# A shorter VectorE program in a grouped-query decode attention kernel: 119 VectorE instructions fewer

## The chip, the cores and the metric

One core of one Trainium2 chip. The metric is the device time of one execution in microseconds (us); lower is better. The profile's span of the same execution is about 2 us shorter than this time, so spans are compared with spans and times with times. The program runs on one core, and all runs told here were in the fast state.

## The reference, cut to what matters

```python
B, Hq, Hkv, Sq, Sk, D = 1, 32, 8, 1, 65536, 128     # bf16
k = repeat(k, 4, axis=1); v = repeat(v, 4, axis=1)   # 4 query heads share one K/V head
scores = einsum("bhqd,bhkd->bhqk", q, k) * D ** -0.5
out = einsum("bhqk,bhkd->bhqd", softmax(scores), v)
```

One query row per head attends to 65,536 keys. K and V together are 268 MB, each byte is used once, and all else is small.

## The kernel before

A "group" g is one of the 8 K/V heads with its 4 query heads. Its K and its V come in two tiles b of 8.4 MB. SBUF holds three tiles at a time: buffer 0 for V, buffers 1 and 2 for the two K tiles of a group. SyncE issues the loads in a fixed order, each behind a wait for the buffer's last reader:

```python
    def load_k(g, b):
        SP.wait((s_sc, 16 * g - 8 + 8 * b if g else 0))   # score matmuls of the old tile are done
        ...  load(k, g, b, 1 + b, ...)
    def load_v(g, b):
        done = 2 * (2 * g + b)
        ...                                               # the last V tiles come in pieces
        else:
            SP.wait((s_vc, done))                         # value matmuls of the old tile are done
            load(v, g, b, 0, s_v[0])
    ...
    for g in range(1, G):
        for b in range(2):
            load_k(g, b)
            load_v(g - 1, b)
```

VectorE transposes each K tile in place, takes the maximum of the scores, prepares the softmax and gathers the result of the group before:

```python
    def transposes(g, b):
        for t0 in range(0, SL, PS):                       # SL = 256, PS = 64: four per tile
            ...
            dve.transpose(out=part.bitcast(u32), in_=part.bitcast(u32)).then_inc(s_kt, 2)
            yield
    def bank_max(g, b):                                   # four per group, 512 columns each
        DV.wait((s_sc, 16 * g + 4 * b + 4))
        return DV.mark(dve.tensor_reduce(out=mx[:, b:b + 1], in_=sc[:, 512 * b:512 * b + 512], ..., op=ALU.max))
    def collect(g):
        n = DV.mark(dve.tensor_scalar_mul(out=vs[:, 0:D], in0=vacc[:, 0, :], scalar1=sely[:, 0:1]))
        ...                                               # copy of the exp sums
        for y in range(1, 4):
            DV.after(n)
            n = DV.mark(dve.scalar_tensor_tensor(out=vs[:, 0:D], in0=vacc[:, y, :], scalar=sely[:, y:y + 1], in1=vs[:, 0:D], ...))
        ...                                               # memset of vacc
    def finish(g):                                        # reciprocal, scaling, a store of 1 KB
        d_rl = reciprocal(pf[0:H, D:D + 1], 3 * g + 7)
        ...
        act.dma_start(out=out[0, g * H:(g + 1) * H, 0, :], in_=o[:, :]).then_inc(s_st, 16)

    for g in range(G):
        ...  # transposes(g, 0); transposes(g, 1) with weights(g - 1, 1) and two bank_max inside
        bank_max(g, 2); DV.after(bank_max(g, 3)); top(); softmax(g)
        if g: DV.wait((s_vc, 4 * g)); collect(g - 1)
        weights(g, 0)
        if g: finish(g - 1)
```

TensorE runs one loop over tiles x = 2g + b: the score matmuls of tile x (8 parts, each behind a share of the transposes), then the value matmuls of tile x - 2, and after each second tile the two small transposes of the softmax.

## Time and profile before

| | before |
|---|---|
| time, median of 3 runs before the prediction (6 with those taken later) | 630.77 us (631.06) |
| loading queue's packets, share of 16 DMA engines' span | 98.9% |
| VectorE busy | 346.9 us, 55% |
| TensorE busy (modelled) | 350.6 us, 56% |

The page of the profile of the kernel before, cut. The row "DMA" has the busy share of the 16 DMA engines in 40 equal slices, in tenths. In the groups below it the last columns are busy us and mean ns of one instruction, then the engine's idle time before them and what ended it.

```profile
span 629.4 us, 6741 instructions
...
PE 350.6 (56%) x2136; PEld 138.0 (22%) x2136; DVE 346.9 (55%) x236; ACT 31.3 (5%) x25; POOL 7.4 (1%) x39
...
DMA  8999999999999999999999999999999999999996
GB/s 367 433 466 400 466 400 463 404 462 404 458 408 458 408 462 404 466 400 467 400 466 400 466 400 466 400 463 404 462 404 462 404 462 404 428 436 433 431 424 248
...
q1 hardware_dynamic: 6624, 268.44, 98.9%
...
q14 instruction: 2, 0.02, 0.0%
...
L225 DVE STREAM_TRANSPOSE io<-io 128x4096 uint32<-128x4096 uint32 x64 | 279.8, 4417 | 152.2 <-DMA io<-in_k_dram 152.2
...
L230 DVE TENSOR_REDUCE mx<-sc 128x1 f32<-128x512 f32 x32 | 20.8, 668 | 48.2 <-PE sc L395 48.2
...
L278 DVE SCALAR_TENSOR_TENSOR vs<-vacc,sely,vs 128x128 f32<-128x128 f32 x24 | 8.4, 351 | 0.6
...
```

The DMA row stands at 9 from the second slice to the last but one: the core is loading all the time. VectorE waits 152.2 us for K tiles, that is, it is ready before its input is there.

The chain of waits that ended last, cut: start, duration, what.

```profile
...
609.60 13.11 DMA io<-in_v_dram
...
622.76 1.45 PE vacc L360 x8
624.21 0.87 PE pf L454 x8
...
625.11 1.38 PE pf L454 x16
...
626.82 0.36 ACT o L323
```

The end of the program hangs on the last V load. After it come 4.5 us of matmuls and a copy, and then the last store.

What could make a slower computing engine cost time is the loading queue running dry (in wide256, below, it does, and the time is 660.02 us). That is read from the timeline, here in the middle of the program (start, duration, engine, line, what; in brackets the idle time before). SPq lines are the issues of loads.

```profile
...
281.98 1.90 PE L360 MATMUL vacc<-io,et 128*16 128x512 bf16 x32
282.09 0.69 DVE L230 TENSOR_REDUCE mx<-sc 128x1 f32<-128x512 f32 x1 [5.74 <-PE sc L395]
...
282.81 0.16 DVE L235 TENSOR_REDUCE mg<-mx 128x1 f32<-128x4 f32 x1
...
286.09 0.33 SPq L132 DMA_DIRECT2D io<-in_v_dram  x1
...
294.65 17.42 DVE L225 STREAM_TRANSPOSE io<-io 128x4096 uint32<-128x4096 uint32 x4 [1.62 <-DMA io<-in_k_dram]
...
300.23 9.55 PE L395 MATMUL sc<-io,wz 128*128 x32 [7.83 <-issue]
...
323.97 0.33 SPq L132 DMA_DIRECT2D io<-in_v_dram  x1
...
333.36 8.77 DVE L225 STREAM_TRANSPOSE io<-io 128x4096 uint32<-128x4096 uint32 x2 [21.28 <-DMA io<-in_k_dram]
...
```

The V load is issued at 286.09, and the K load in flight then has landed at 294.65, when its transposes start: 8.6 us of margin. The next V load is issued at 323.97, and the K load ahead lands at 333.36: 9.4 us.

### The profile page before, as it was taken

What the parts mean: (1) busy time and instruction counts of PE and PEld (TensorE: products, weight loads), DVE (VectorE), ACT (ScalarE), POOL (GpSimd) and SP (SyncE); (2) the same over time, 40 slices, a digit from 0 to 9 for tenths busy, and PEclk for the clock granted to TensorE, in tenths of its full rate; (3) what the DMA queues carried; (4) which work ended last, traced back from release to release, by engine and by line L of the source; (5) the groups of instructions that cost most, each with busy time, mean ns of one, the idle gap of its engine ahead of it and who ended that gap; (6) DMA issues with size and microseconds to landing.
All of it is one profiled execution on the core that took longest, in us unless ns stands there. A gap on an engine that the chain in (4) does not pass through costs nothing. (4 is left out here: it accounts for less than half of the span.)

```text
span 629.4 us, 6741 instructions
## 1 busy us (share of the span) xinstructions
PE 350.6 (56%) x2136; PEld 138.0 (22%) x2136; DVE 346.9 (55%) x236; ACT 31.3 (5%) x25; POOL 7.4 (1%) x39
## 2 busy tenths in 40 slices
PE   0676582736627375372854719457184571886435
PEld 0222130312213122130321303123031230332102
DVE  4993926649066590765808567084670947684200
ACT  0000100020000200002000020000200002000100
POOL 1000000000000000000000000000000000000000
PEclk9999595977959779697896968869698696999577
DMA  8999999999999999999999999999999999999996
GB/s 367 433 466 400 466 400 463 404 462 404 458 408 458 408 462 404 466 400 467 400 466 400 466 400 466 400 463 404 462 404 462 404 462 404 428 436 433 431 424 248
DMA packets 6739, 268.49 MB, mean 427 GB/s; under 512 B 848, under 2 KB 1104, under 8 KB 1488
## 3 DMA queue, kind: packets, MB, share of 16 engines
q1 hardware_dynamic: 6624, 268.44, 98.9%
q10 hardware_dynamic: 112, 0.02, 0.0%
q8 instruction: 1, 0.02, 0.0%
q14 instruction: 2, 0.02, 0.0%
HBM read 268.44 MB, written 0.01 MB: 427 GB/s over the span
## 5 line engine op out<-in xcount | busy, mean ns | idle before, releaser
L395 PE MATMUL sc<-io,wz 128*128 x1024 | 268.2, 412 | 205.7 <-PEq L114 108.9
L225 DVE STREAM_TRANSPOSE io<-io 128x4096 uint32<-128x4096 uint32 x64 | 279.8, 4417 | 152.2 <-DMA io<-in_k_dram 152.2
L395 PEld LDWEIGHTS sc<-io,wz 128*128 x1024 | 104.8, 102 | 369.2 <-issue 290.9
L360 PE MATMUL vacc<-io,et 128*16 128x512 bf16 x1018 | 70.9, 411 | 21.6 <-PEq L114 20.2
L230 DVE TENSOR_REDUCE mx<-sc 128x1 f32<-128x512 f32 x32 | 20.8, 668 | 48.2 <-PE sc L395 48.2
L249 ACT ACTIVATE ex<-sc,nmb 128x2048 bf16<-128x2048 f32 x8 | 15.8, 1969 | 560.9 <-DVE nmb L247 560.9
L360 PEld LDWEIGHTS vacc<-io,et 128*16 128x16 bf16 x1018 | 27.4, 94 | 60.0 <-issue 35.5
L266 DVE STREAM_TRANSPOSE et<-ex 128x512 bf16<-128x512 bf16 x32 | 20.6, 681 | 16.6 <-PE vacc L360 14.2
L354 PE MATMUL pf<-vs,sel 128*4 128x129 f32 (+1 forms) x20 | 5.7, 386 | 42.0 <-PEq L114 42.0
L239 DVE TENSOR_REDUCE m<-pt 1x4 f32<-1x128 f32 x8 | 2.2, 278 | 30.8 <-PE pt L438 30.8
L257 ACT ACTIVATE sc<-zero 128x2048 f32<-128x2048 f32 x7 | 13.2, 1882 | 0.3
L340 POOL COPY wz<-qT 32x16 bf16<-32x16 bf16 x32 | 6.1, 191 | 516.5 <-PE sc L395 454.3
L354 PEld LDWEIGHTS pf<-vs,sel 128*4 128x4 f32 x20 | 1.2, 83 | 42.4 <-issue 42.4
L273 DVE TENSOR_SCALAR vs<-vacc,sely 128x128 f32<-128x128 f32 x8 | 2.7, 343 | 13.5 <-PE vacc L360 13.5
L422 PE MATMUL pt<-et 128*16 128x512 bf16 x32 | 9.7, 384 | 0.0
L278 DVE SCALAR_TENSOR_TENSOR vs<-vacc,sely,vs 128x128 f32<-128x128 f32 x24 | 8.4, 351 | 0.6
L270 DVE RECIPROCAL rl<-pf 4x1 f32<-4x1 f32 x7 | 1.0, 149 | 10.0 <-PE pf L354 10.0
L440 PE MATMUL pb<-one,nrow 1*128 1x1 f32 x8 | 1.6, 196 | 5.7 <-PEq L114 5.7
L284 DVE MEMSET vacc<- 128x512 f32 x7 | 3.4, 485 | 1.3 <-DVE vs L278 1.3
L422 PEld LDWEIGHTS pt<-et 128*16 128x16 bf16 x32 | 3.0, 93 | 4.1 <-issue 0.6
L247 DVE COPY nmb<-pb 128x1 f32<-128x1 f32 x8 | 1.3, 159 | 3.0 <-PE pb L440 3.0
L438 PE MATMUL pt<-ident,mg 128*1 128x128 f32 x8 | 2.3, 282 | 1.1 <-PEq L114 1.1
(30 smaller groups left out, 22.3 us busy)
## 6 DMA issues: line engine op xcount, KB each, us to landing
io<-in_v_dram SPq DMA_DIRECT2D x5, 4096.0 KB, 16.1
io<-in_k_dram SPq DMA_DIRECT2D x4, 4096.0 KB, 26.0
io<-in_k_dram SPq DMA_DIRECT2D x4, 2048.0 KB, 39.0
io<-in_v_dram SPq DMA_DIRECT2D x1, 2048.0 KB, 11.0
io<-in_v_dram SPq DMA_DIRECT2D x1, 1024.0 KB, 13.1
io<-in_v_dram SPq DMA_DIRECT2D x3, 256.0 KB, 13.5
io<-in_v_dram SPq DMA_DIRECT2D x2, 128.0 KB, 13.4
io<-in_k_dram SPq DMA_DIRECT2D x13, 47.2
```

What stands on the lines that cost most here:

```text
L225: dve.transpose(out=part.bitcast(u32), in_=part.bitcast(u32)).then_inc(s_kt, 2)
L230: return DV.mark(dve.tensor_reduce(out=mx[:, b:b + 1], in_=sc[:, 512 * b:512 * b + 512], axis=AX.X, op=ALU.max))
L249: n = ACTQ.mark(act.activation(out=ex[:, :, :].rearrange("p b n -> p (b n)"), in_=sc[:, :], func=ACT.Exp, bias=nmb[:, :], scale=SCALE, acc ...
L257: cleared[g] = ACTQ.mark(act.activation(out=sc[:, :], in_=zero[:, 0:1].to_broadcast([P, 4 * 512]), func=ACT.Copy))
L266: dve.transpose(out=et[:, i, :], in_=ex[:, 2 * b + i, :]).then_inc(s_et, 1)
L278: n = DV.mark(dve.scalar_tensor_tensor(out=vs[:, 0:D], in0=vacc[:, y, :], scalar=sely[:, y:y + 1], in1=vs[:, 0:D], op0=ALU.mult, op1=ALU.a ...
L284: n = DV.mark(dve.memset(vacc[:, :, :], 0.0))
L340: gp.tensor_copy(out=wz[r, :, c0:c0 + H].rearrange("p (s w) h -> p s w h", s=2), in_=qTb[r, :, :, g, :],).then_inc(s_w, 1)
L354: return pe.matmul(out=pf[0:H, 0:w], lhsT=sel[:, :], rhs=vs[:, 0:w], skip_group_check=True, **kw)
L360: return pe.matmul(out=vacc[32 * c:32 * c + 16, :, :], lhsT=et[:, ch // 2, w0:w0 + 16], rhs=io[:, PS * ch + 4 * tt:PS * ch + 4 * tt + 4, : ...
L395: i = pe.matmul(out=bass.AP(sc, r_o, [[2048, P], [1, 512]]), lhsT=bass.AP(wz, r_w + ((2 * s + e) * WB - 4 * u), [[4 * WB, P], [1, P]]), rh ...
L422: pe.matmul(out=pt[0:16, :], lhsT=et[:, 0, 0:16], rhs=et[:, 0, :], start=True, stop=True,)
```

## The change

Its intent is to relieve VectorE: one maximum per group over all 2048 columns, one product and one row sum where four multiply-adds stood, exp sums written where they are needed, both halves of the weights transposed by one instruction, wider K transposes in groups 2 to 6, the clearing of the accumulator moved to ScalarE, and one store for seven heads' groups at the end. The core of the diff (cuts marked by `...`):

```diff
     def transposes(g, b):
-        for t0 in range(0, SL, PS):
...
+            n = 128 if 1 < g < G - 1 and b == 0 else 64
+            for t in range(t0, t0 + 128, n):
...
+                dve.transpose(out=part, in_=part).then_inc(s_kt, n // 32)
             yield
-    def bank_max(g, b):
...
-    def top():
-        dve.tensor_reduce(out=mg[:, :], in_=mx[:, :], axis=AX.X, op=ALU.max).then_inc(s_mg, 1)
+    def top(g):
+        DV.wait((s_sc, 16 * g + 16))
+        dve.tensor_reduce(out=mg[:, :], in_=sc, axis=AX.X, op=ALU.max).then_inc(s_mg, 1)
...
-            bias=nmb[:, :], scale=SCALE, accum_out=ls[:, g % 2:g % 2 + 1],
+            bias=nmb[:, :], scale=SCALE, accum_out=vs[:, D + g % 2:D + g % 2 + 1],
...
+    def clear(g):
+        cleared[g] = ACTQ.mark(act.activation(
+            out=acc[:, :], in_=wz[:, 0, 0:1].to_broadcast([P, 5 * 512]), func=ACT.Copy
+        ))
...
-    def collect(g):
-    ...
-    def finish(g):
-    ...
+    def collect():
+        n = DV.mark(dve.tensor_tensor(
+            out=vy[:, :, :], in0=vacc, in1=sely[:, :, None].to_broadcast([P, 4, D]), op=ALU.mult
+        ))
+        DV.after(n)
+        return DV.mark(dve.tensor_reduce(
+            out=vs[:, 0:D], in_=vy[:, :, :].rearrange("p y d -> p d y"), axis=AX.X, op=ALU.add
+        ))
+    def keep(g):
+        ACTQ.wait((s_pe, 3 * g + 7))
+        return ACTQ.mark(act.activation(out=fall[:, g, :], in_=pf[0:H, 0:D + 2], func=ACT.Copy))
...
+    o7 = io[0:H, SL:SL + G - 1, :]
...                                     (two reciprocals and one product for seven groups)
+    sp.dma_start(
+        out=out[0, 0:(G - 1) * H, 0, :].rearrange("(g h) d -> h g d", h=H), in_=o7
+    ).then_inc(s_st, 16)
```

More of the change, by code (lines that the diff above doesn't have):

```diff
@@ L75 @@
     wz = sb("wz", [P, 4, WB], bf16)
-    zero = sb("zero", [P, 1], fp32)
     ident = sb("ident", [P, P], fp32)
@@ L82 @@
     sely = sb("sely", [P, 4], fp32)
-    one = sb("one", [1, 1], fp32)
-    mx = sb("mx", [P, 4], fp32)
     mg = sb("mg", [P, 1], fp32)
@@ L88 @@
     nmb = sb("nmb", [P, 1], fp32)
-    ls = sb("ls", [P, 2], fp32)
     rl = sb("rl", [H, 1], fp32)
@@ L92 @@
     et = sb("et", [P, 2, 512], bf16)
-    vs = sb("vs", [P, D + 1], fp32)
+    vs = sb("vs", [P, D + 2], fp32)
+    vy = sb("vy", [P, 4, D], fp32)
+    fall = sb("fall", [H, G - 1, D + 2], fp32)
+    r7 = sb("r7", [H, G - 1], fp32)
     o = sb("o", [H, D], bf16)
-    sc = ps("sc", [P, 4 * 512])
-    vacc = ps("vacc", [P, 4, D])
+    acc = ps("acc", [P, 5 * 512])
+    sc, vacc = acc[:, 0:2048], acc[:, 2048:2560].rearrange("p (y d) -> p y d", d=D)
     pt = ps("pt", [P, 512])
@@ L154, in load_v @@
             SP.wait((s_vc, done))
+            for s in s_v[2:4]:
+                down(sp, mybir.EngineType.SP, s, 16)
             for lo, hi, s in list(zip(CUTS, CUTS[1:], s_v))[1:]:
@@ L181 @@
     GP.mark(gp.memset(wz[:, :, :], 0.0))
+    GP.mark(gp.memset(vs[:, :], 0.0))
     n = GP.mark(gp.memset(ident[:, :], 0.0))
@@ L187 @@
     ))
-    DV.mark(dve.memset(one[:, :], 1.0))
-    d_zero = DV.mark(dve.memset(zero[:, :], 0.0))
-    DV.mark(dve.memset(vs[:, :], 0.0))
-    for b in range(4):
-        DV.mark(dve.memset(sc[:, 512 * b:512 * b + 512], 0.0))
-    n = DV.mark(dve.memset(vacc[:, :, :], 0.0))
+    n = DV.mark(dve.memset(acc[:, :], 0.0))
     collected = {-2: n, -1: n}
@@ L220, in transposes @@
     def transposes(g, b):
-        for t0 in range(0, SL, PS):
+        for t0 in range(0, SL, 128):
             if (g, b, t0) in k_ready:
                 DV.wait(k_ready[g, b, t0])
-            part = io[:, (1 + b) * SL + t0:(1 + b) * SL + t0 + PS, :].rearrange("p t d -> p (t d)")
-            dve.transpose(out=part.bitcast(u32), in_=part.bitcast(u32)).then_inc(s_kt, 2)
-            yield
-    def bank_max(g, b):
-        DV.wait((s_sc, 16 * g + 4 * b + 4))
-        return DV.mark(dve.tensor_reduce(
-            out=mx[:, b:b + 1], in_=sc[:, 512 * b:512 * b + 512], axis=AX.X, op=ALU.max
-        ))
-    def top():
-        dve.tensor_reduce(out=mg[:, :], in_=mx[:, :], axis=AX.X, op=ALU.max).then_inc(s_mg, 1)
+            n = 128 if 1 < g < G - 1 and b == 0 else 64
+            for t in range(t0, t0 + 128, n):
+                if t > t0 and (g, b, t) in k_ready:
+                    DV.wait(k_ready[g, b, t])
+                part = io[:, (1 + b) * SL + t:(1 + b) * SL + t + n, :]
+                part = part.rearrange("p t d -> p (t d)").bitcast(u32)
+                dve.transpose(out=part, in_=part).then_inc(s_kt, n // 32)
+            yield
+    def top(g):
+        DV.wait((s_sc, 16 * g + 16))
+        dve.tensor_reduce(out=mg[:, :], in_=sc, axis=AX.X, op=ALU.max).then_inc(s_mg, 1)
     def softmax(g):
@@ L249, in softmax @@
         n = ACTQ.mark(act.activation(
-            out=ex[:, :, :].rearrange("p b n -> p (b n)"), in_=sc[:, :], func=ACT.Exp,
-            bias=nmb[:, :], scale=SCALE, accum_out=ls[:, g % 2:g % 2 + 1],
+            out=ex[:, :, :].rearrange("p b n -> p (b n)"), in_=sc, func=ACT.Exp,
+            bias=nmb[:, :], scale=SCALE, accum_out=vs[:, D + g % 2:D + g % 2 + 1],
         ))
+        exped[g] = n
         if g == 0:
-            ACTQ.wait((s_dv, d_zero))
-        if g < G - 1:
+            ACTQ.wait((s_gp, p_ident))
@@ L256, in softmax @@
             ACTQ.after(n)
-            cleared[g] = ACTQ.mark(act.activation(
-                out=sc[:, :], in_=zero[:, 0:1].to_broadcast([P, 4 * 512]), func=ACT.Copy
-            ))
+            clear(0)
+    def clear(g):
+        cleared[g] = ACTQ.mark(act.activation(
+            out=acc[:, :], in_=wz[:, 0, 0:1].to_broadcast([P, 5 * 512]), func=ACT.Copy
+        ))
+    exped = {}
     cleared = {}
     def weights(g, b):
-        for i in range(2):
-            DV.wait((s_ac, 2 * g + 1))
-            dve.transpose(out=et[:, i, :], in_=ex[:, 2 * b + i, :]).then_inc(s_et, 1)
@@ L268, in reciprocal @@
-    def reciprocal(src, n_pe):
-        DV.wait((s_pe, n_pe))
-        return DV.mark(dve.reciprocal(out=rl[:, :], in_=src))
-    def collect(g):
-        n = DV.mark(dve.tensor_scalar_mul(out=vs[:, 0:D], in0=vacc[:, 0, :], scalar1=sely[:, 0:1]))
-        if g < G - 1:
-            DV.mark(dve.tensor_copy(out=vs[:, D:D + 1], in_=ls[:, g % 2:g % 2 + 1]))
-        for y in range(1, 4):
-            DV.after(n)
-            n = DV.mark(dve.scalar_tensor_tensor(
-                out=vs[:, 0:D], in0=vacc[:, y, :], scalar=sely[:, y:y + 1], in1=vs[:, 0:D],
-                op0=ALU.mult, op1=ALU.add,
-            ))
-        if g < G - 1:
-            DV.after(n)
-            n = DV.mark(dve.memset(vacc[:, :, :], 0.0))
-        collected[g] = n
@@ L287, in finish @@
-    def finish(g):
-        d_rl = reciprocal(pf[0:H, D:D + 1], 3 * g + 7)
-        DV.wait((s_st, 16 * g))
-        DV.after(d_rl)
-        n = DV.mark(dve.tensor_scalar_mul(out=o[:, :], in0=fin, scalar1=rl[:, :]))
-        ACTQ.wait((s_dv, n))
-        act.dma_start(out=out[0, g * H:(g + 1) * H, 0, :], in_=o[:, :]).then_inc(s_st, 16)
+        if b == 0:
+            DV.wait((s_ac, exped[g]))
+        dve.transpose(
+            out=et[:, :, :].rearrange("p i n -> p (i n)"),
+            in_=ex[:, 2 * b:2 * b + 2, :].rearrange("p i n -> p (i n)"),
+        ).then_inc(s_et, 1)
@@ L298 @@
         for i, _ in enumerate(transposes(g, 1)):
-            if i == 1:
-                if g:
-                    DV.wait((s_vc, 4 * g - 2))
-                    weights(g - 1, 1)
-                bank_max(g, 0)
-                bank_max(g, 1)
-        bank_max(g, 2)
-        DV.after(bank_max(g, 3))
-        top()
-        softmax(g)
-        if g:
-            DV.wait((s_vc, 4 * g))
-            collect(g - 1)
-        weights(g, 0)
-        if g:
-            finish(g - 1)
-    DV.wait((s_vc, 4 * G - 2))
-    for s in s_v[2:4]:
-        down(dve, mybir.EngineType.DVE, s, 16)
-    weights(G - 1, 1)
+            if i == 0 and g:
+                DV.wait((s_vc, 4 * g - 2))
+                weights(g - 1, 1)
+        top(g)
+        softmax(g)
+        if 0 < g < G - 1:
+            weights(g, 0)
+            DV.wait((s_vc, 4 * g))
+            collected[g - 1] = collect()
+            ACTQ.wait((s_dv, collected[g - 1]))
+            clear(g)
+        elif g:
+            DV.wait((s_vc, 4 * g))
+            DV.after(collect())
+            collected[g - 1] = DV.mark(dve.memset(vacc, 0.0))
+            weights(g, 0)
+        else:
+            weights(g, 0)
+        if g:
+            n_kept = keep(g - 1)
+    DV.wait((s_ac, n_kept), (s_vc, 4 * G - 2))
+    weights(G - 1, 1)
+    o7 = io[0:H, SL:SL + G - 1, :]
+    for i in range(2):
+        n = DV.mark(dve.reciprocal(out=r7[:, i::2], in_=fall[:, i::2, D + i]))
+    DV.after(n)
+    n = DV.mark(dve.tensor_tensor(
+        out=o7, in0=fall[:, :, 0:D], in1=r7[:, :, None].to_broadcast([H, G - 1, D]),
+        op=ALU.mult,
+    ))
+    SP.wait((s_dv, n))
+    sp.dma_start(
+        out=out[0, 0:(G - 1) * H, 0, :].rearrange("(g h) d -> h g d", h=H), in_=o7
+    ).then_inc(s_st, 16)
     DV.wait((s_vb, 2 * G))
-    collect(G - 1)
-    d_rl = reciprocal(pl, 3 * G + 2)
-    ACTQ.wait((s_st, 16 * (G - 1)), (s_dv, d_rl), (s_pe, 3 * G + 3))
+    collected[G - 1] = collect()
+    DV.wait((s_pe, 3 * G + 2))
+    d_rl = DV.mark(dve.reciprocal(out=rl[:, :], in_=pl))
+    ACTQ.wait((s_dv, d_rl), (s_pe, 3 * G + 3))
     n = ACTQ.mark(act.activation(out=o[:, :], in_=fin, func=ACT.Copy, scale=rl[:, :]))
@@ L325 @@
     act.dma_start(out=out[0, (G - 1) * H:G * H, 0, :], in_=o[:, :]).then_inc(s_st, 16)
-    ACTQ.wait((s_st, 16 * G))
+    ACTQ.wait((s_st, 32))
     for g in range(G):
@@ L338 @@
             if a == 3:
-                GP.wait((s_dv, collected[g - 2]), (s_ac, cleared.get(g - 1, 0)))
+                GP.wait(
+                    (s_dv, collected[g - 2]), (s_ac, cleared.get(g - 1, 0))
+                )
             gp.tensor_copy(
@@ L343 @@
             ).then_inc(s_w, 1)
-    GP.wait((s_sc, 16 * G), (s_dv, collected[G - 2]))
+    GP.wait((s_sc, 16 * G), (s_dv, collected[G - 2]), (s_ac, exped[G - 1]))
     gp.sem_inc(s_w, 4)
@@ L377 @@
         take(s_w, 4)
-        gather(D + 1, start=True, stop=True).then_inc(s_pe, 1)
+        gather(D + 2, start=True, stop=True).then_inc(s_pe, 1)
         nc.br("pe_tile", engines=only)
@@ L395 @@
                     i = pe.matmul(
-                        out=bass.AP(sc, r_o, [[2048, P], [1, 512]]),
+                        out=bass.AP(acc, r_o, [[2560, P], [1, 512]]),
                         lhsT=bass.AP(wz, r_w + ((2 * s + e) * WB - 4 * u), [[4 * WB, P], [1, P]]),
@@ L407 @@
     with block("pe_values"):
-        take(s_et, 2)
+        take(s_et, 1)
         for ch in range(4):
@@ L440 @@
         pe.transpose(
-            out=pb[:, 0:1], in_=nrow[:, :, :].rearrange("o x h -> o (x h)"), identity=one[:, :]
+            out=pb[:, 0:1], in_=nrow[:, :, :].rearrange("o x h -> o (x h)"), identity=ident[0:1, 0:1]
         ).then_inc(s_pe, 1)
@@ L448 @@
             pe.matmul(
-                out=pl, lhsT=sel[:, :], rhs=ls[:, (G - 1) % 2:(G - 1) % 2 + 1], start=True, stop=True
+                out=pl, lhsT=sel[:, :], rhs=vs[:, D + (G - 1) % 2:D + (G - 1) % 2 + 1],
+                start=True, stop=True,
             ).then_inc(s_pe, 1)
```

## The prediction

> **What bounds the kernel now.** The loads of K and V. The page's DMA lines: 268.44 MB read, 427 GB/s over the 629.4 us span, the loading queue busy for 98.9% of 16 engines' span. A 64 KB packet takes 2.42 us (packet records): 433.6 GB/s for 16 engines, all in flight from 2 to 623 us. [...] At that packet time the bytes need 619 us (estimate: 4096 packets / 16 x 2.418). The rest is a 2 us head and a tail: in the chain of waits the last V load lands at 622.7 us, then come matmuls, a copy and the last store. VectorE: 55% busy.
>
> **What the change does.**
> - Row maximum per group: 4 x 0.668 + 0.157 = 2.83 us becomes one reduction. [...] Starting after the last score matmul, [...]hidden behind 4 us of value matmuls (281.98 to 286.0 us, timeline).
> - Collect: 0.343 + 3 x 0.351 + 0.145 + 0.485 = 2.0 us [...]; the clearing goes to ScalarE (1.88 us grows to about 2.35).
> - Reciprocal and scaling (0.49 us) move to the end; seven stores become one.
> - In groups 2 to 6, twenty of the 64 K transposes (4.40 us each) become ten of about 8.75 us. Those tiles' first score matmul starts about 4.4 us later.
>
> VectorE busy: 347 to an estimated 331 to 337 us.
>
> **How much is on the critical path.** Almost none. What counts is whether the load queue runs dry. Issues come in pairs of a V and a K load (286.09/286.52, 323.97/324.40 us), each 8.6 to 9.4 us before the load ahead has landed (transposes begin at 294.65 and about 333.4). The later start takes about 4.4 us of one of these two margins and leaves 5 us: no gap. [...] The seven-head store lands before the last store. A possible gain is fewer small transfers between loads (two instruction fetches of 0.31 us at 107 and 415 us, seven stores): at most 0.5 us.
>
> **Prediction.** 630.5 us, with 629.5 to 631.6 holding it 8 times in 10. Faster by over 2%: 0.01; within 2%: 0.97; slower by over 2%: 0.02.
>
> **What would show it.** DMA still about 98.9% busy; last V landing at 622 to 624 us; VectorE busy down by 10 to 16 us and its wait for K (152.2 us) up by as much; [...]first score matmul of groups 2 to 6 about 10 us after K lands instead of 5.6; that half's V issues 4.4 us later, yet no dip in the DMA row.
>
> **What would make it wrong.** A smaller margin than I read: if the queue drains, each of five groups loses microseconds (645 us or more). [...] A gain over 1 us would mean that stores or instruction fetches disturb the loads more than their size says.

The forecast's sum: VectorE busy for 331 to 337 us, which is 10 to 16 us less. Of the terms only the reciprocal and scaling, 7 x 0.49 = 3.4 us moved out of the groups, can be followed. The forecast of the time, 630.5 us, rests on the loads and the margins. Of the estimates, 2.35 us for the clearing is 1.88 us scaled from 2048 to 2560 columns (measured after: 2.31), and 8.75 us for a wide transpose is about twice 4.40 (measured after: 8.69).

## The result, and the profile after

| | before | after |
|---|---|---|
| time, median of 6 runs each (lowest to highest) | 631.06 us (630.62 to 632.39) | 630.08 us (629.92 to 630.91) |
| VectorE busy | 346.9 us | 339.2 us |
| VectorE idle before K transposes | 152.2 us | 161.2 us |
| last packet of K and V ends (packet records) | 624.88 us | 624.23 us |

The ratio after over before is 0.9985, with a 95% interval from 0.9972 to 0.9998. Ratios here are the mean time of one kernel's fast runs over that of the other's of the same rounds, so they are not quite the ratios of the medians quoted. 0.15% faster, about 0.9 us.

The same lines of the page after the change:

```profile
span 628.0 us, 6627 instructions
...
PE 352.5 (56%) x2136; PEld 138.0 (22%) x2136; DVE 339.2 (54%) x131; ACT 36.1 (6%) x32; POOL 7.5 (1%) x40
...
DMA  8999999999999999999999999999999999999996
GB/s 368 434 459 409 459 409 459 409 451 417 451 417 451 417 443 426 442 426 434 434 430 438 422 447 417 451 405 463 401 463 405 463 405 463 399 434 434 434 432 277
...
q1 hardware_dynamic: 6656, 268.45, 99.1%
...
q14 instruction: 2, 0.01, 0.0%
...
L227 DVE STREAM_TRANSPOSE io<-io 128x4096 uint32<-128x4096 uint32 (+1 forms) x54 | 279.0, 5207 | 161.2 <-DMA io<-in_k_dram 161.2
...
L232 DVE TENSOR_REDUCE mg<-acc 128x1 f32<-128x2048 f32 x8 | 18.3, 2291 | 55.4 <-PE acc L405 55.4
...
L278 DVE TENSOR_REDUCE vs<-vy 128x128 f32<-128x512 f32 x8 | 8.2, 1021 | 0.3
...
```

VectorE is busy 7.7 us less and waits 9.0 us longer for K. The trace holds 280 records of VectorE before and 161 after; the page's x236 and x131 leave out its semaphore waits, drains and a branch. The loading queue is as full as before. The one maximum takes 2.29 us, the row sum 1.02 us. One line on the right track is easily passed over: the queue q14, which carries instruction fetches. It moved 0.02 MB before and 0.01 MB after; of its two packets after, one has only 40 bytes, at the very start.

The chain after, cut:

```profile
...
610.09 13.25 DMA io<-in_v_dram
...
623.38 0.61 PE pf L465 x8
...
624.04 1.06 PE pf L465 x16
...
625.43 0.36 ACT o L331
```

It has the same parts: a 13 us V load, then the narrow matmuls, a copy and the store. The two profiled spans differ by 1.4 us, and not all of that is the loads. The loads end 0.65 us earlier; what follows them is 4.50 us long before and 3.77 us after. That second difference goes with the granted TensorE clock: `--windows` gives 0.60 and 0.67 of full speed for 622.00 to 624.80 and 624.80 to 626.60 us before, and 1.00 in the last microseconds after (622.00 to 625.40), and most of the last narrow matmuls start 107 ns apart before and 56 ns after. The profile of stores7 has a tail at the low clock too (0.54, 4.69 us); in the other kernels it is 3.7 to 3.9 us (stores56 and loads_only, which end differently, aside). So the tail can add about 0.8 us to a single run, and the medians have to be compared, not the two profiles. Why the clock was lower there is not known.

The timeline after, the same stretch of the program:

```profile
...
281.47 1.90 PE L370 MATMUL acc<-io,et 128*16 128x512 bf16 x32
281.57 2.29 DVE L232 TENSOR_REDUCE mg<-acc 128x1 f32<-128x2048 f32 x1 [6.76 <-PE acc L405]
...
285.57 0.33 SPq L131 DMA_DIRECT2D io<-in_v_dram  x1
...
294.96 17.30 DVE L227 STREAM_TRANSPOSE io<-io 128x8192 uint32<-128x8192 uint32 x2 [3.15 <-DMA io<-in_k_dram]
...
304.80 7.20 PE L405 MATMUL acc<-io,wz 128*128 x24 [9.59 <-issue]
...
328.54 0.33 SPq L131 DMA_DIRECT2D io<-in_v_dram  x1
...
333.66 8.77 DVE L227 STREAM_TRANSPOSE io<-io 128x4096 uint32<-128x4096 uint32 x2 [21.39 <-DMA io<-in_k_dram]
...
```

The maximum at 281.57 ends at 283.86, while value matmuls run on to 285.5, so its 1.4 us longer way to the end is hidden. The first K tile of a group lands at 294.96; its first score matmul starts 9.84 us later instead of 5.58, behind the first 8.7 us transpose (two of them are merged in this line). The V issue moves to 328.54, 5.1 us before the next K tile has landed at 333.66. The margin shrinks as predicted and is not used up.

### The profile page after: what moved, and what is told of

Its sections match the earlier page's. It is cut to its first block, busy times and chain, and to the rows that moved or that the text cites. A ratio compares the mean times of both kernels' runs of the same rounds, so it can differ in the third digit from the quotient of the medians.

```text
span 628.0 us, 6627 instructions
## 1 busy us (share of the span) xinstructions
PE 352.5 (56%) x2136; PEld 138.0 (22%) x2136; DVE 339.2 (54%) x131; ACT 36.1 (6%) x32; POOL 7.5 (1%) x40
## 5 line engine op out<-in xcount | busy, mean ns | idle before, releaser
L405 PE MATMUL acc<-io,wz 128*128 x1024 | 270.7, 416 | 179.7 <-issue 92.2
L227 DVE STREAM_TRANSPOSE io<-io 128x4096 uint32<-128x4096 uint32 (+1 forms) x54 | 279.0, 5207 | 161.2 <-DMA io<-in_k_dram 161.2
L405 PEld LDWEIGHTS acc<-io,wz 128*128 x1024 | 105.5, 103 | 345.0 <-issue 267.4
L370 PE MATMUL acc<-io,et 128*16 128x512 bf16 x1018 | 70.6, 409 | 22.3 <-PEq L113 20.9
L232 DVE TENSOR_REDUCE mg<-acc 128x1 f32<-128x2048 f32 x8 | 18.3, 2291 | 55.4 <-PE acc L405 55.4
L246 ACT ACTIVATE ex<-acc,nmb 128x2048 bf16<-128x2048 f32 x8 | 15.7, 1967 | 531.1 <-DVE nmb L244 531.1
L370 PEld LDWEIGHTS acc<-io,et 128*16 128x16 bf16 x1018 | 27.4, 94 | 61.1 <-issue 36.5
L268 DVE STREAM_TRANSPOSE et<-ex 128x1024 bf16<-128x1024 bf16 x16 | 19.6, 1225 | 30.0 <-PE acc L370 15.1
L257 ACT ACTIVATE acc<-wz 128x2560 f32<-128x2560 bf16 x7 | 16.1, 2307 | 17.7 <-DVE vs L278 17.6
L236 DVE TENSOR_REDUCE m<-pt 1x4 f32<-1x128 f32 x8 | 2.2, 279 | 21.7 <-PE pt L448 21.7
L278 DVE TENSOR_REDUCE vs<-vy 128x128 f32<-128x512 f32 x8 | 8.2, 1021 | 0.3
```

The costliest lines, as they stand in the source:

```text
L227: dve.transpose(out=part, in_=part).then_inc(s_kt, n // 32)
L232: dve.tensor_reduce(out=mg[:, :], in_=sc, axis=AX.X, op=ALU.max).then_inc(s_mg, 1)
L246: n = ACTQ.mark(act.activation(out=ex[:, :, :].rearrange("p b n -> p (b n)"), in_=sc, func=ACT.Exp, bias=nmb[:, :], scale=SCALE, accum_out ...
L257: cleared[g] = ACTQ.mark(act.activation(out=acc[:, :], in_=wz[:, 0, 0:1].to_broadcast([P, 5 * 512]), func=ACT.Copy))
L268: dve.transpose(out=et[:, :, :].rearrange("p i n -> p (i n)"), in_=ex[:, 2 * b:2 * b + 2, :].rearrange("p i n -> p (i n)"),).then_inc(s_et, 1)
L278: return DV.mark(dve.tensor_reduce(out=vs[:, 0:D], in_=vy[:, :, :].rearrange("p y d -> p d y"), axis=AX.X, op=ALU.add))
```

## The experiments

**Theory.** The load stream bounds the time; VectorE, whichever way it is arranged, is off the critical path as long as V issues come before the queue is empty. The small gain comes from instruction fetches: a shorter VectorE program needs one fetch less while the loads run, a fetch uses one of the 16 DMA engines, and the last load waits for the slowest engine.

**Rivals.** The gain comes from the seven small stores that went; or from VectorE's shorter busy time; or it is noise.

The fetches are seen in the packet records of the trace. "Long packets" are all 64 KB packets of the loads over 2.8 us; the median is 2.42.

```
                fetches of 8 KB (q14) during     long packets: start us, ns
                the loads: start us, ns
before          106.81 309;  415.05 332          41.60 3053; 107.12 3056; 415.37 3080
after           223.24 309                       41.32 3548; 41.78 3338; 223.55 3059; 254.66 3027
loads_only      none                             none
fetch1          106.89 309;  415.02 331          41.77 3633; 107.20 3059; 415.34 3080
```

Each fetch of the table is followed, at the moment that it ends, by one load packet of 3.06 to 3.08 us instead of 2.42 (in all runs: 2.80 to 3.08 us after each fetch that comes before the last group). So a fetch takes one engine not 0.31 us but about 0.31 + 0.64 = 0.95 us of its load time. The records do not name the engine, but its packets can be followed, since each starts within 10 ns of the end of the one before. From the fetch at 106.81 us to that at 415.05 us in the kernel before, 152 such steps lead without a fork, so both fall on the same engine; in fetch1 the same holds (144 steps), and in fetch7 for the first five fetches (110 steps). At the end, one engine alone has load packets for the last 1.07 us in the kernel before, 0.64 us in fetch1 and 0.12 us in the changed kernel. (Long packets at about 41 us occur with hardly any exception in the kernels that compute, and not in the loads alone; their cause, and that of single ones such as the one at 254.66, was not looked for.)

All twelve runs are told below. The first four ran on one chip, the next four on a second, the loads alone on a third, the last three on a fourth. In this table "fetches" are those of 8 KB on q14 between the first and the last load packet, in the profiled run, and "loads end" is the end of the last load packet of K and V there.

| kernel | fetches | loads end, us | time, median us | ratio to before [95%] |
|---|---|---|---|---|
| before | 2 | 624.88 | 631.06 | |
| after | 1 | 624.23 | 630.08 | 0.9985 [0.9972, 0.9998] |
| after_again | 1 | 624.13 | 630.25 | 0.9991 [0.9978, 1.0005] |
| stores7 | 1 | 624.06 | 630.21 | 0.9982 [0.9969, 0.9996] |
| fetch1 | 2 | 624.78 | 630.98 | 0.9999 [0.9986, 1.0013] |
| n64 | 1 | 623.91 | 630.10 | 0.9982 [0.9969, 0.9996] |
| fetch7 | 8 | 632.85 | 638.54 | 1.0119 [1.0102, 1.0135] |
| stores56 | 2 | 625.36 | 632.77 | 1.0027 [1.0010, 1.0044] |
| wide256 | 1 | 653.95 | 660.02 | 1.0463 [1.0446, 1.0481] |
| vec9 | 1 | 624.17 | 630.71 | 0.9999 [0.9983, 1.0016] |
| loads_only (wrong result) | 0 | 623.00 | 628.25 | 0.9953 [0.9936, 0.9969] |
| after_third | 1 | 624.61 | 630.24 | 0.9989 [0.9975, 1.0002] |
| vec9b | 1 | 624.26 | 630.23 | 0.9990 [0.9976, 1.0004] |
| stores24 | 1 | 624.74 | 630.94 | 0.9997 [0.9984, 1.0011] |

### after_again: the changed kernel, unedited, as a yardstick

> The changed kernel once more, as the yardstick on this chip. Theory (loads bound the time; what little is gained comes from one instruction fetch less during the run, each fetch slowing one DMA engine by about 0.65 us, which the last load has to wait for): 0.9985 of the kernel before, about 0.5 to 1 us less; one 8 KB fetch in the packet records, last V packet about 0.7 us earlier. Rival 'noise': a ratio whose interval holds 1. Rival 'VectorE time counts': also about 0.9985, so this run alone does not tell them apart.

Measured: 630.25 us against 631.3 of the kernel before; the interval of the ratio holds 1. One fetch, at 223.17 us. The gain is of the size of the noise, and a single comparison does not settle it; three such comparisons gave 0.9985, 0.9991 and 0.9989. All runs together are clearer: of the 40 runs of kernels whose profile has one fetch (the changed kernel, stores7, n64, vec9 and stores24), 23 are faster than the fastest of the 43 runs with two (the kernel before and fetch1: 630.56 us), and the means are 0.75 us apart.

### stores7: the seven small stores put back

```diff
-    def keep(g): ...                              # ScalarE copy into fall
+    def finish(g):                                # reciprocal and scaling per group on VectorE
+        ...
+        act.dma_start(out=out[0, g * H:(g + 1) * H, 0, :], in_=o[:, :]).then_inc(s_st, 16)
-    o7 = ...                                      # and the store of seven groups
```

> The changed kernel with the seven stores of the kernel before put back (reciprocal and scaling on VectorE per group, one small store each), but still only one instruction fetch expected. Fetch theory: equal to the changed kernel within 0.3 us (four packets of 18 ns per store). Rival 'small stores disturb the loads': the gain is lost, about 631 us, as the kernel before.

Measured: 630.21 us, ratio 0.9982, one fetch. With the stores back and the second fetch still away, the gain stays. The rival of the small stores falls as the main cause. (The profiled run of stores7 is its slowest, 630.91 us, with the tail at the low clock; its loads end at 624.06 us. In the packet records of the kernel before, each of the seven small stores is four packets of 256 bytes and 18 ns.)

### fetch1: as many VectorE instructions as before

The kernel's trace has 280 records of VectorE, as many as before the change.

```diff
+        if g:
+            for j in range(17):
+                dve.memset(pad[:, (g - 1) * 17 + j:(g - 1) * 17 + j + 1], 0.0)
         for i, _ in enumerate(transposes(g, 1)):
```

> The changed kernel with 119 one-element memsets on VectorE (17 in each of seven groups, in its wait for the group's second K tile), so that its program is as long as before. Fetch theory: a second 8 KB fetch appears during the run and the time rises by about 0.65 us to that of the kernel before. Rival 'small stores' or 'VectorE busy time': no change against the changed kernel (the memsets add about 7 us of VectorE work in a wait).

Measured: 630.98 us, ratio 0.9999, and two fetches at 106.89 and 415.02 us, nearly where the kernel before has them. On this chip the 15 runs of the three one-fetch kernels (after_again, stores7, n64) have a mean of 630.35 us, the five of fetch1 631.18, the nine of the kernel before 631.26. The gain is gone with nothing else of the change undone. The memsets raise VectorE's busy time only from 339.2 to 340.7 us: the expected 7 us is 119 times the 59 ns that a one-element memset lasts in the kernel before.

### n64: narrow K transposes

```diff
-            n = 128 if 1 < g < G - 1 and b == 0 else 64
+            n = 64
```

> The changed kernel with all K transposes of 64 rows again (64 instructions, no wide ones). Load theory: V issues of groups 2 to 6 return to 323.97 us and the like, 4.4 us earlier, and the time does not change (within 0.5 us of the changed kernel), since the queue never drains in either. Rival 'the later issue costs part of the gain': faster than the changed kernel by 1 us or more.

Measured: 630.10 us; V issues at 324.04 us and the like, 4.5 us earlier than in the changed kernel. Using or not using half of the margin makes no difference that these runs resolve.

### fetch7: a dose of seven more fetches

```diff
+        if g:
+            for j in range(128):
+                ... dve.memset(pad[y:y + 1, x % 224:x % 224 + 1], 0.0)   # one element each
         for i, _ in enumerate(transposes(g, 1)):
```

> The changed kernel with 896 one-element memsets on VectorE (128 in each of seven groups, in its wait for the group's second K tile): a dose of seven more 8 KB instruction fetches. Fetch theory: if every fetch slows the same DMA engine by 0.65 us, 4.5 us more than the changed kernel, about 634.6 us; if fetches are spread over engines, less. Rival 'fetches cost nothing': unchanged, as the memsets (about 55 us in all) lie in a wait of 21 us per group.

Measured: 638.54 us, about 8.3 us over the changed kernel, which ran on other chips, and 7.6 us over the kernel before on the same chip, for six fetches more. The page of fetch7, cut:

```profile
span 636.6 us, 7523 instructions
...
PE 350.0 (55%) x2136; PEld 137.4 (22%) x2136; DVE 360.8 (57%) x1027; ACT 36.1 (6%) x32; POOL 7.5 (1%) x40
...
q14 instruction: 8, 0.07, 0.0%
...
```

VectorE's busy time rises by only 21.6 us (the 896 memset records last 59 ns each, 52.9 us in sum, but overlap to 21.7), and eight fetches are counted. The memsets do fall in waits: those of the group in the middle end at 318.2 us, 18.9 us before the next transposes, and the V issue comes 33.6 us after its K tile has landed (331.00 against 297.41), as in the changed kernel. The packet records show the form of the cost: at the end only one engine still has load packets to move from 630.69 to 632.85 us, while all 16 are at work until 628.52. A packet of 3.02 to 3.08 us follows each of the seven fetches before the last group. Seven fetches at 0.95 us are 6.7 us, so the expected 4.5 was too low because it left out the fetch itself, and 1.6 us more are not explained by that sum. They may come from the engine's growing lag, if every load's landing, and with it the next issue, waits for the slowest engine: clusters of 9 to 14 long packets appear at 332, 410 and 488 us, as they do in wide256, where the queue runs dry. The records do show engines without a load packet there, for 2.0 us in all up to 620 us against 0.1 in the changed kernel (counted as for wide256 below). That the lag is the reason is argued, not shown.

### stores56: a dose of small stores that went wrong

```diff
             n_kept = keep(g - 1)
+            for j in range(8):
+                ACTQ.wait((s_pd, 16 * (8 * (g - 1) + j)))
+                act.dma_start(out=out[0, (G - 1) * H:G * H, 0, :], in_=pad[:, :]).then_inc(s_pd, 16)
...
-    ACTQ.wait((s_dv, d_rl), (s_pe, 3 * G + 3))
+    ACTQ.wait((s_pd, 16 * 8 * (G - 1)), (s_dv, d_rl), (s_pe, 3 * G + 3))
```

> The changed kernel with eight extra small stores (4 x 256 bytes, zeros, overwritten at the end by the right values) after each of seven groups, one after another: a dose of eight times the seven stores that the change removed. Fetch theory (stores cost 18 ns a packet): under 1 us more than the changed kernel. Rival 'small stores disturb the loads, 0.9 us for seven': about 7 us more, 637 us.

Measured: 632.77 us, 2.5 to 2.7 over the changed kernel, which neither theory expected. The chain of waits that ended last, cut, shows why:

```profile
...
594.80 6.07 DMA out_dram<-pad
...
606.97 6.05 DMA out_dram<-pad
...
626.20 1.15 DMA out_dram<-pad
...
627.37 1.16 DMA out_dram<-pad
...
```

The last eight stores, one waiting for the other, became the end of the program themselves, since the edit's last line lets the final copy wait for them: under load one takes 4 to 6 us from issue to landing, after the loads 1.15 us. In addition there was a second fetch at 463 us, probably of ScalarE's program, which had grown by 56 stores (it had 63 records by then). The run measures its own tail and says little of the stores' effect on the loads, except that these end only 1.1 us later than in the changed kernel, with 56 stores and one more fetch.

### wide256: one transpose for a whole K tile in groups 2 to 6

```diff
-        for t0 in range(0, SL, 128):
+        wide = 1 < g < G - 1 and b == 0
+        for t0 in range(0, SL, 256 if wide else 128):
...
-            n = 128 if 1 < g < G - 1 and b == 0 else 64
+            n = 256 if wide else 64
```

> The changed kernel with the first K tile of groups 2 to 6 transposed by one instruction of 256 rows (17.3 us). Load theory with the margin as read (V issued about 5 us before the queue drains in the changed kernel): the issue comes 8.7 us later still, so the queue stands empty for about 3.7 us plus some 2 us until data flows again, in each of five groups: 18 to 28 us more, 648 to 658 us, with dips in the DMA row. If the margin was read wrong and is larger than 8.7 us: unchanged.

Measured: 660.02 us, 4.6% slower than the kernel before and about 30 us over the changed kernel. A line of the page of wide256: the DMA row now has dips:

```profile
...
DMA  9999999999799998899987999979999699899997
...
```

And its timeline in the middle, VectorE and the load issues:

```profile
...
306.99 17.25 DVE L228 STREAM_TRANSPOSE io<-io 128x16384 uint32<-128x16384 uint32 x1 [8.13 <-DMA io<-in_k_dram]
345.68 8.77 DVE L228 STREAM_TRANSPOSE io<-io 128x4096 uint32<-128x4096 uint32 x2 [21.45 <-DMA io<-in_k_dram]
...
349.08 0.33 SPq L131 DMA_DIRECT2D io<-in_v_dram  x1
...
```

The tile of 306.99 is now handed to TensorE in one piece after 17.25 us. The V load is issued at 349.08, but the K load ahead has landed at 345.68: the queue has been empty for 3.4 us. The packet records have 27.9 us in which an engine was without a load packet (a sixteenth of a microsecond counted for each engine and microsecond), against 1.3 in the changed kernel; divided among five groups, 5.3 us each. This is 3.4 us of lateness, and the remaining 1.9 us, by difference, pass until data flows again. The expected 18 to 28 us was slightly too low, but the margin was read rightly: 4.5 us of delay cost nothing between n64 and the changed kernel, and 8.5 us more (the issue comes 42.1 us after the landing of the tile before, not 33.6) cost 6 us of time per group.

### vec9 and vec9b: more VectorE work in a wait

```diff
+        if g:
+            dve.tensor_reduce(
+                out=pad[:, :], in_=ident[:, None, :].to_broadcast([P, 64, P]), axis=AX.XY, op=ALU.max
+            )
         for i, _ in enumerate(transposes(g, 1)):
```

> The changed kernel with one reduction over 8192 columns (an estimated 8.6 us) in each of seven groups, in VectorE's wait for the second K tile: VectorE busy from 339 to about 399 us, seven instructions more. Load theory: no change (within 0.5 us of the changed kernel). Rival 'VectorE busy time counts': it rises by a good part of 60 us; if time followed the 7.7 us that the change took off VectorE for a gain of 0.9 us, by about 7 us.

Measured: 630.71 us, but in two clusters, 630.12 and 630.16 against 631.26 and 631.36, and without the changed kernel on the same chip: inconclusive at half a microsecond, though far from 7 us. So it was repeated beside the changed kernel, which ran there as after_third.

> The changed kernel again, as the yardstick on this chip for the next two. Fetch theory: one 8 KB fetch during the run, last packet of the loads at about 624.1 us, 0.999 of the kernel before.

> The kernel with one 8192-column reduction more in each of seven groups, repeated beside the changed kernel on the same chip, because the first time had no such neighbour and its runs fell into two clusters (630.1 and 631.3 us). Load theory: within 0.5 us of the changed kernel. Rival 'VectorE busy time counts, 0.9 us for 7.7': about 7 us more.

Measured: after_third 630.24 us, vec9b 630.23 us. A line of the page of vec9b:

```profile
...
PE 351.7 (56%) x2136; PEld 137.5 (22%) x2136; DVE 399.0 (64%) x138; ACT 36.1 (6%) x32; POOL 7.5 (1%) x40
...
```

VectorE works 60 us more (seven reductions of 8.64 us each), from 54% to 64% of the span, and the time does not move. VectorE's busy time is no reason for the gain.

### stores24: the dose of stores, mended

```diff
             n_kept = keep(g - 1)
+        if 0 < g < G - 1:
+            ACTQ.wait((s_pd, 16 * 4 * (g - 1)))
+            for j in range(4):
+                act.dma_start(out=out[0, j * H:(j + 1) * H, 0, :], in_=pad[:, :]).then_inc(s_pd, 16)
...                                     (the seven-head store waits for these stores)
```

> The dose of small stores mended: four extra stores of zeros to different rows after each of groups 1 to 6 (24 in all, 3.4 times the seven that were removed), none in the tail, and few enough that ScalarE's program should need no further fetch. Fetch theory: one fetch, within 0.4 us of the changed kernel. Rival 'small stores disturb the loads, 0.9 us for seven': 3 us more.

Measured: 630.94 us against 630.24 for after_third, with one fetch. That is 0.7 us for 24 stores, more than the 0.4 that the theory allowed and far below the rival's 3 us; the intervals of the two ratios overlap. At 0.03 us a store, the seven removed stores would be worth 0.2 us, an amount that stores7 could not show.

### loads_only: the loads without any computation

The kernel keeps the loads, their order, sizes and cuts. Each waits only for the earlier load into the same part of its buffer. One store of zeros ends it, so its result is wrong.

```diff
-            SP.wait((s_vc, done))            # and the like: waits for computing engines
+        for l, h, sm, n in past[at]:         # waits for the earlier load there
+            if l < hi and h > lo:
+                sp.wait_ge(sm, n)
```

> Wrong result on purpose: the same loads of K and V in the same order, sizes and cuts, each waiting only for the earlier load into the same part of its buffer, no computation, one store of zeros at the end. Load theory: 625 to 627 us: 2 us until the first packet, 621 to 622 us of loads at 2.42 us a 64 KB packet, 2 us for the store, so that no change to the computing engines can gain more than about 4 us. Rival 'computation slows the loads': well below, 620 us or less.

Measured: 628.25 us, a span of 626.0. The expected 625 to 627 us fits the span and misses the time, since the 2 us between the two was forgotten. (Of its parts, the first load packet starts at 1.97 us in the kernel before, and the last store there takes 2.2 us from its issue to the end of the span; in loads_only 3.0 us lie between the end of the loads and the end of the span.) Lines of its page (the GB/s row in the same 40 slices, and the loading queue):

```profile
...
GB/s 368 435 469 402 469 402 469 402 469 402 452 419 440 431 402 469 402 469 402 469 402 469 402 469 402 469 402 452 419 435 435 402 469 402 434 427 445 436 429 308
...
q1 hardware_dynamic: 6624, 268.44, 99.4%
...
```

No fetch occurs during the loads, no 64 KB packet is over 2.8 us, and the loads end at 623.00 us, 1.2 us before those of the changed kernel. The swing in the GB/s row is there without any computation. The changed kernel is 0.3% above its own loads; no rearrangement of the computing engines could have gained more than about 3 us on the kernel before. No version that beats both kernels came out of the experiments: n64 and stores7 are equal to the changed kernel within noise.

## Why the prediction was right

The stated range, 629.5 to 631.6 us, also holds the time of the kernel before, 631.06 us, so that the hit alone says little. The mechanism was tested by the runs:

- **What bounds the kernel** was right. The loads alone take 628.25 us of 631, and 60 us of added VectorE work cost nothing (vec9b).
- **The way to the maximum**: the one maximum takes 2.29 us where the last two reductions took 0.88 us before (282.09 to 282.97), and the difference is hidden behind value matmuls.
- **The margin** was right: the V issue came 4.6 us later (328.54 against 323.97), leaving 5.1 us, and wide256 showed what lies beyond it.
- **The tail** had no room left: product and row sum, 0.69 and 1.03 us there, end at 624.89 us, as the last narrow matmul starts (624.88), and the matmul that gathers their result starts at 624.95. In the profile of fetch1 that matmul starts 0.20 us after the last narrow one, so it waits there for the row sum. The seven-head store was in time: its packets end at 624.22 us, and those of the last store start at 626.57.
- **VectorE's saving** was mis-sized: 7.7 us instead of 10 to 16. Collecting a group costs 0.66 + 1.02 = 1.68 us on VectorE, before 2.0 with the clearing. I took the row sum, 1.02 us, for the term at fault; that rested on the estimate that is cut, and is not shown.
- **The possible gain from fewer small transfers**, "at most 0.5 us", was mis-sized too. I added the fetches' own durations, 0.31 us each. The runs showed about 0.95 us per fetch on one DMA engine, since the next load packet is 0.64 us longer, and by my theory the last load waits for that engine: at the end one engine alone has load packets, for 1.07 us before the change and 0.12 us after it; that it is the engine of the fetches fits, but the records do not show it. One fetch less is most of the 0.7 to 1.0 us that separate the medians: in the profiled pair the loads end 0.65 us earlier. What is left may be chance in the clock of the tail; that was not shown. Dose (fetch7), restoration (fetch1) and removal to zero (loads_only, which removes all other work too) agree in direction; the sizes, 8.3 us for seven and about 0.8 for one, are not exactly proportional.

Open: why seven fetches cost a quarter more than seven times 0.95 us, why the clock in the tail differs between executions, and whether small stores cost 0 or 0.03 us each.

## What to carry to other kernels

Where the loads kept the DMA engines busy, as here (98.9% of 16 engines' span), busy time on another engine was not a cost: 60 us more of it on VectorE did not move the time (vec9b). Ask by how many microseconds each buffer is given back before the queue runs dry, and watch that margin when instructions are merged, because a merged instruction hands over its result later: with transposes twice as wide the first score matmul started 9.84 us after its tile had landed instead of 5.58, which the margin covered; with transposes four times as wide the queue ran dry and the time was 660.02 us (wide256). In this kernel even instruction fetches were traffic: each took about 0.95 us of one DMA engine's load time, and seven more came with 8.3 us more, which the profile shows only in the queue lines and packet records. Test a cause that is smaller than the noise by multiplying it, and see to it that the dose does not build a new tail, as eight chained stores did here.
